# Linear attention feeding a tanh-shrink MoE on one core: a quarter of q issued by SyncE, transposes copied late, 1/den of two head pairs split into bf16 parts by GpSimd, batch 1 reordered

## The chip, the cores and the metric

The kernel runs on one core of one Trainium2 chip. The metric is the device time of one execution in microseconds (us). Unless a number is called a median of runs, it is a start or a length in the profiled execution of the kernel named, in microseconds from the start of that execution's span; the span is about 1.8 us shorter than the device time. In the lines of profiles PE is TensorE, DVE VectorE, ACT ScalarE, POOL GpSimd and SP SyncE; PSUM is the memory, in eight banks, in which TensorE's results lie, and a load "lands" when its data is there.

## The reference

```python
# q, k, v: 8 batches x 8 heads x 576 tokens x 64;  w_in: 512 x 2048;  w_out: 2048 x 512
phi = lambda x: np.where(x > 0, x, np.exp(x) - 1.0) + 1.0
q_p, k_p = phi(q), phi(k)
kv  = np.einsum('bhsd,bhse->bhde', k_p, v)
z   = np.sum(k_p, axis=2)
num = np.einsum('bhsd,bhde->bhse', q_p, kv)
den = np.einsum('bhsd,bhd->bhs', q_p, z)[..., None] + 1e-06
x   = (num / den).transpose(0, 2, 1, 3).reshape(4608, 512)
h   = x @ w_in
out = (h - np.tanh(h)) @ w_out
```

## The kernel before

The kernel works through the 4608 tokens in nine chunks of 512, `c` = 0 to 8. A chunk is 64 matmuls with `w_in` ("L1": 16 blocks `fi` of four) and 64 with `w_out` ("L2": 16 steps of four), each 0.216 us when TensorE runs dense. The attention of the next batches is worked in between: `s1[fi]` holds what follows block `fi` of L1, `s2[s]` what follows step `s` of L2. So the order of the program text is the order of each engine's work. Attention of a batch is: exp and phi of q and k (ScalarE, VectorE), transposes of phi(q) (TensorE, copied out of PSUM by ScalarE or VectorE), kv and z, den, its reciprocal, num, and the scaling of num by 1/den into `xT`, from which L1 reads.

The opening, and the work of batch 1 in chunk 0 (cuts marked):

```python
load_q(0)                      # two halves, each one transfer issued by GpSimd, cast float32 -> bf16
load_k(0)
make_identity(nc, ident)
load_v(0)
for f0, n in (...): load_wi(f0, n)
load_k(1); load_wo(0); load_wo(1); load_q(1)
...                            # memsets by GpSimd
load_v(1); load_wo(2); load_wo(3)
...
spin(18)                       # dummy matmuls while q lands
a_qT_pe(0, 0, side, "AV")      # transposes; copies by ScalarE and VectorE
... # phi(k)
spin(5)
a_qT_pe(0, 1, side, "AA")
... # z, kv, den of batch 0
b0_spread((0, 2), 0)           # 1/den spread over partitions, float32 matmuls
b0_scale(0, ns0, 0); b0_scale(2, ns0, 1)
b0_num(1, ns0)
def open2():                   # called after the first two L1 matmuls of chunk 0
    b0_spread((1, 3), 2)
    b0_scale(1, ns0, 2); b0_scale(3, ns0, 3)
...
s2[7].append(lambda: (a_qT_pe(1, 0, side), a_qT_pe(1, 1, side), a_kv(1, side)))
s2[8].append(lambda: b0_scale_rest(side))
s2[9].append(lambda: a_den(1, side))
s2[10].append(lambda: (num1(), a_split(1)))
s2[11].append(lambda: spread1(0))
```

Chunk 1 makes batch 2. Its `vp` is v of batch 2 in another layout, and its 1/den goes through DRAM and is broadcast back (`rdb`):

```python
s1[7 if c == 1 else 5].append(lambda: a_kv_cols(n1, attn))                     # needs vp
s1[10 if c == 1 else 8].append(lambda: (a_den(n1, attn), a_spread(n1)))       # den, 1/den, broadcast
for p in range(NP + 1):
    s2[(11 if c == 1 else 9) + p].append(lambda p=p: a_num(n1, p))             # needs the broadcast
if c == 1:
    s1[1].append(lambda: a_kphi(2, 1))
    for i in range(2):
        s1[3].append(lambda i=i: a_vp(2, i))
if c >= 1 and n2 < B:
    s1[0].append(lambda: (gate(qT_t[n1]), load_k(n2), load_q(n2), load_v(n2)))
```

Of the kernel before, what the change touches and what calls it, by code (L numbers as in the profile page):

```python
# [18 lines left out]
def kernel(  # L19
# [65 lines left out]
    def load(b, t, src, halves):  # L85

        x = src[b].rearrange("h (p j) d -> (h p) (j d)", j=J)
        if halves:
            for i in range(2):
                nc.gpsimd.dma_start(out=t[:, :, i].rearrange("q h j d -> q h (j d)"),  # L90
                                    in_=x.rearrange("(h i q) x -> i q h x", h=2, i=2)[i])
        else:
            nc.gpsimd.dma_start(out=t.rearrange("q h i j d -> q (h i) (j d)"),  # L93
                                in_=x.rearrange("(n q) x -> q n x", n=4))
# [26 lines left out]
    def phi_pieces(b, src, store, name, i, parts=0):  # L121
# [7 lines left out]
        if parts:  # L129

            return ([lambda h=h: nc.scalar.activation(e[:, h], x[:, h], AF.Exp) for h in range(2)],
                    lambda: nc.vector.tensor_scalar(r, x, 0.0, 1.0, ALU.max, ALU.add),
                    [lambda h=h: nc.vector.tensor_tensor(y[:, h], e[:, h], r[:, h], ALU.min) for h in range(2)])
# [37 lines left out]

    def kv_mm(b, i, ps):
# [15 lines left out]
    def a_vp(b, i):  # L188
        nc.vector.tensor_copy(vp[:, i, :, 0:128].rearrange("p j (h d) -> p h j d", h=2), v_b[b % 2][:, 0:2, i])

# [14 lines left out]
    def b0_z(i):  # L205

        for j in range(J):
            for hg in range(2):
                r = slice(64 * hg, 64 * hg + 64)
                nc.tensor.matmul(ps_all[:, 4 - 2 * i + hg, 0:32], kp_t[0][r, i, j].rearrange("p h d -> p (h d)"),  # L210
                                 one[r, 0:32], start=(j == 0), stop=(j == J - 1))

    def b0_zc(i):
        nc.vector.tensor_mul(kz_t[0][:, :, i, 128:160], ps_all[:, 4 - 2 * i:6 - 2 * i, 0:32], mask[:, :, i, 128:160])

    def b0_kv(i):

        for j in range(J):
            for hg in range(2):
                r = slice(64 * hg, 64 * hg + 64)  # L220
                nc.tensor.matmul(ps_all[:, 2 * i + hg, 0:128], kp_t[0][r, i, j].rearrange("p h d -> p (h d)"),
                                 v_b[0][r, 0:2, i, j, :], start=(j == 0), stop=(j == J - 1))

    def b0_kz(i):
        nc.vector.tensor_mul(kz_t[0][:, :, i, 0:128], ps_all[:, 2 * i:2 * i + 2, 0:128], mask[:, :, i, 0:128])

    def b0_num(i, ns):
# [5 lines left out]
        nc.scalar.copy(ns[:, i::2, 0:8, :].rearrange("p a j t -> p a (j t)"), ps_all[:, b0:b0 + 2, :])  # L233

# [172 lines left out]
    nc.scalar.activation(act0, zero[:, 0:1], AF.Exp)  # L407
    load_q(0)
# [5 lines left out]
    load_k(1)  # L414
    load_wo(0)
    load_wo(1)
    load_q(1)
    for i in (1, 0):
        nc.gpsimd.memset(v_b[i][:, 2], 1.0)
    nc.gpsimd.memset(vp[:, :, :, 128:136], 1.0)  # L420
    load_v(1)
    load_wo(2)
    load_wo(3)

# [20 lines left out]

    side = Banks([4, 5, 6, 7])
    kz_t[0] = kz_c[0]
    (eq0, rq0, mq0), (eq1, rq1, mq1) = (phi_pieces(0, q_t, qp_t, "qp", i) for i in range(2))
    for f in (eq0, rq0, mq0, eq1, rq1, mq1):
        f()  # L450
    spin(18)
    a_qT_pe(0, 0, side, "AV")
    (ek0, rk0, mk0), (ek1, rk1, mk1) = (phi_pieces(0, k_t, kp_t, "kp", i, 2 * i) for i in range(2))
# [3 lines left out]
    a_qT_pe(0, 1, side, "AA")  # L457

    for t in range(4):
        nc.scalar.copy(s8[32 * t:32 * t + 32, 0].rearrange("q h p -> q (h p)"),  # L460
                       ident[32 * t:32 * t + 32, 32 * t:32 * t + 8])
    nc.scalar.copy(sel, s8[:, 0].rearrange("q h p -> q p h").unsqueeze(3).to_broadcast([128, NP, 2, 64]))
    spin(6)
# [3 lines left out]
    b0_zc(0)  # L467
    b0_kv(0)
    b0_kz(0)
    b0_z(1)  # L470
    b0_zc(1)
    a_den(0, Banks([4]))
    ns0 = new_ns(0)
# [9 lines left out]
    def open2():  # L483
        b0_spread((1, 3), 2)
        b0_scale(1, ns0, 2)
        b0_scale(3, ns0, 3)

    def prepare():

        for t in range(4):  # L490
            nc.vector.tensor_copy(s8[32 * t:32 * t + 32, 1:3].rearrange("q n h p -> q (n h p)"),
                                  ident[32 * t:32 * t + 32, 32 * t + 8:32 * t + 24])
        s24 = rpool.tile([128, 2 * NP], F32, name="s24")
        f8 = s8.rearrange("q n h p -> q n (h p)")
        nc.vector.tensor_add(s24, f8[:, 1], f8[:, 2])
# [147 lines left out]
```

## Time and profile before

The time is 294.82 us, the median of three runs (294.65 to 294.93). Five points cut the first 85 us into parts.

| point | before, us | how it is read |
|---|---|---|
| k's second half in use | 10.46 | first exp of k in two pieces on ScalarE |
| dense stream starts | 17.64 | the row of 62 L1 matmuls on TensorE |
| transposes of batch 1 start | 37.94 | the row with ident,qp |
| chunk 1 starts | 51.30 | the next row of L1 matmuls |
| chunk 2 starts | 82.12 | the same, one chunk on |

From VectorE's timeline of the kernel before (start, length, line, operation, output and input, idle time in front and what ended it):

```profile
64.37 1.05 DVE L285 RECIPROCAL rden<-den 128x144 f32<-128x144 f32 x1
79.10 1.89 DVE L328 TENSOR_TENSOR xT<-ps_all,rdb 128x512 bf16<-128x512 f32 x3 [2.26 <-DMA rdb<-ds]
```

And from TensorE's:

```profile
62.60 0.43 PE L276 MATMUL ps_all<-qT,kz 128*32 128x144 bf16 x16
...
78.73 0.38 PE L317 MATMUL ps_all<-qT,kz 128*128 128x512 bf16 x1
...
79.85 0.38 PE L317 MATMUL ps_all<-qT,kz 128*128 128x512 bf16 x1
```

1/den of batch 2 is ready at 65.42, and its broadcast is in use at 79.10, in the first of the scalings: VectorE waits for it. The num matmuls of a batch share two PSUM banks, so the third needs the bank that the first scaling frees; that scaling takes 0.69 us, to 79.79, and the third num matmul starts at 79.85, 0.04 later than the step of 1.08 between the first two would bring it.

### The profile page before, as it was taken

The numbers are of one execution on the slowest core, as the hardware profiler recorded it, in microseconds if no ns is written. First come the engines' busy times: TensorE is split into PE (matmuls) and PEld (weight loads), VectorE is DVE, ScalarE is ACT, GpSimd is POOL, SyncE is SP. The second block draws the span as 40 slices with busy tenths as digits, with TensorE's granted clock in tenths as the row PEclk, the third lists the DMA queues.
The fourth block names the chain that finished last, engine by engine and source line by source line (L and its number), as shares of the span: only waits on it lengthen the run. The fifth ranks groups of instructions, "written<-read, shape, count | busy, mean of one in ns | idle before, by whom it ended". The sixth has DMA issues, their size and how long they took to land.

```text
span 293.2 us, 4504 instructions
## 1 busy us (share of the span) xinstructions
PE 285.2 (97%) x1801; PEld 134.3 (46%) x1801; DVE 174.6 (60%) x265; ACT 139.6 (48%) x168; POOL 33.3 (11%) x55
## 2 busy tenths in 40 slices
PE   8899999999999999999999999999999999999994
PEld 2544453454444444444444445444444444444443
DVE  4759857887567764786478646865581456106600
ACT  4938536947344643455246524661552155126411
POOL 8673030030030003000300020000000000000000
PEclk9999999999999999999999999999999999999999
DMA  6999999998999758955895669667117310131032
GB/s 101 194 204 212 208 207 216 200 145 153 234 163 185 160 118 139 218 117 129 136 223 127 139 134 183 134 154 143 38 24 178 73 36 0 38 84 24 0 74 72
DMA packets 39077, 38.94 MB, mean 133 GB/s; under 512 B 16336, under 2 KB 33808, under 8 KB 38288
## 3 DMA queue, kind: packets, MB, share of 16 engines
q0 software_dynamic: 17552, 18.35, 38.6%
q1 hardware_dynamic: 21344, 20.17, 30.3%
q8 instruction: 14, 0.23, 0.3%
q10 hardware_dynamic: 160, 0.13, 0.1%
q14 instruction: 7, 0.06, 0.1%
HBM read 43.91 MB, written 9.55 MB: 182 GB/s over the span
## 4 chain that ended last, share of the span: by engine, by line
PE 79%; DMA 11%; issue 7%; POOL 2%; DVE 0%; ACT 0%; POOLq 0%
PE ps_all L387 37%; PE ps_all L366 36%; DMA qraw<-in_q_dram 6%; DMA w_in_sb<-in_moe_w_in_dram 3%; PE ps_all L199 2%; DMA kraw<-in_k_dram 2%; PE ps_all L317 2%; PE ps_all L604 1%; PE ps_all L276 1%; POOL qraw L90 0%; ACT e L134 0%; POOL kraw L93 0%; DVE qp L136 0%; POOL v L93 0%; POOL w_out_sb L115 0%
## 5 line engine op out<-in xcount | busy, mean ns | idle before, releaser
L366 PE MATMUL ps_all<-xT,w_in_sb 128*128 128x512 bf16 x576 | 128.0, 379 | 0.3 <-DVE xT L244 0.3
L387 PE MATMUL ps_all<-w_out_sb,gT 128*128 128x512 bf16 x560 | 127.8, 379 | 0.0
L373 DVE TENSOR_TENSOR gT<-ps_all,th 128x1024 bf16<-128x1024 f32 x64 | 77.9, 1218 | 59.8 <-ACT th L372 59.8
L372 ACT ACTIVATE th<-ps_all 128x1024 f32<-128x1024 f32 x64 | 65.5, 1024 | 57.0 <-PE ps_all L366 47.1
L366 PEld LDWEIGHTS <-w_in_sb 128*128 128x128 bf16 x576 | 55.3, 98 | 66.6 <-issue 0.6
L387 PEld LDWEIGHTS <-gT 128*128 128x128 bf16 x560 | 54.1, 98 | 64.3 <-issue 0.3
L396 ACT COPY osb<-ps_all 128x512 f32<-128x512 f32 (+1 forms) x36 | 20.9, 583 | 73.4 <-PE ps_all L387 54.2
L328 DVE TENSOR_TENSOR xT<-ps_all,rdb 128x512 bf16<-128x512 f32 x24 | 16.3, 689 | 13.4 <-PE ps_all L317 11.2
L134 ACT ACTIVATE e<-qraw 128x1152 bf16<-128x1152 bf16 x16 | 18.5, 1162 | 6.9 <-DMA qraw<-in_q_dram 6.9
L134 ACT ACTIVATE e<-kraw 128x1152 bf16<-128x1152 bf16 x15 | 17.5, 1166 | 0.2 <-DMA kraw<-in_k_dram 0.2
L136 DVE TENSOR_TENSOR qp<-e,r 128x1152 bf16<-128x1152 bf16 x16 | 12.0, 757 | 7.8 <-ACT e L134 7.2
L136 DVE TENSOR_TENSOR kp<-e,r 128x1152 bf16<-128x1152 bf16 x15 | 11.4, 759 | 8.3 <-ACT e L134 7.5
L383 POOL COPY g<-qT 1x1 bf16<-1x1 bf16 x5 | 1.2, 240 | 120.6 <-DMA qT<-qp 120.6
L378 DVE TENSOR_TENSOR gT<-ps_all,th 128x512 bf16<-128x512 f32 x16 | 10.3, 685 | 2.4 <-ACT th L377 1.7
L377 ACT ACTIVATE th<-ps_all 128x512 f32<-128x512 f32 x16 | 9.2, 598 | 4.3 <-PE ps_all L366 3.1
L317 PE MATMUL ps_all<-qT,kz 128*128 128x512 bf16 x28 | 10.1, 379 | 0.0
L444 PE MATMUL ps_all<-zero 128*128 128x512 bf16 x29 | 8.8, 463 | 1.2 <-DVE zero L405 1.2
L135 DVE TENSOR_SCALAR r<-qraw 128x1152 bf16<-128x1152 bf16 x16 | 7.3, 453 | 2.2 <-DMA qraw<-in_q_dram 2.2
L199 PE MATMUL ps_all<-vp,kp 64*128 64x136 bf16 x216 | 7.4, 220 | 0.4 <-POOL g L383 0.4
L199 PEld LDWEIGHTS <-kp 64*128 64x128 bf16 x216 | 6.4, 94 | 3.0 <-issue 2.1
L285 DVE RECIPROCAL rden<-den 128x144 f32<-128x144 f32 x7 | 7.4, 1053 | 0.2
L394 DVE COPY osb<-ps_all 128x128 f32<-128x128 f32 x1 | 0.3, 292 | 11.6 <-PE ps_all L604 11.6
(82 smaller groups left out, 121.7 us busy)
## 6 DMA issues: line engine op xcount, KB each, us to landing
out_dram<-osb SPq DMA_DIRECT2D x70, 128.0 KB
rdb<-ds SPq DMA_DIRECT2D x12, 576.0 KB
kraw<-in_k_dram POOLq DMA_DIRECT2D x7, 576.0 KB, 7.1
qraw<-in_q_dram POOLq DMA_DIRECT2D x7, 576.0 KB, 9.0
v<-in_v_dram POOLq DMA_DIRECT2D x7, 576.0 KB, 12.2
w_out_sb<-in_moe_w_out_dram POOLq DMA_DIRECT2D x4, 512.0 KB, 16.4
w_in_sb<-in_moe_w_in_dram POOLq DMA_DIRECT2D x6, 256.0 KB, 8.6
qraw<-in_q_dram POOLq DMA_DIRECT2D x2, 288.0 KB, 4.6
```

What stands on the lines that cost most here:

```text
L134: return (lambda: nc.scalar.activation(e, x, AF.Exp), lambda: nc.vector.tensor_scalar(r, x, 0.0, 1.0, ALU.max, ALU.add), lambda: nc.vector ...
L136: lambda: nc.vector.tensor_tensor(y, e, r, ALU.min))
L199: nc.tensor.matmul(ps[hg][:, i, :], kp[r, i, j].rearrange("p h d -> p (h d)"), vp[r, i, j, :], start=(j == 0), stop=(j == J - 1))
L317: nc.tensor.matmul(ps, kz[:, p // 2, p % 2, 0:128], qT[:, p % 2, 0:8, p // 2, :], start=True, stop=True)
L328: nc.vector.tensor_mul(xT[:, p, S * b:S * b + 512].rearrange("p (j t c) -> p j t c", j=8, t=4), ps.rearrange("p j (t c) -> p j t c", t=4), ...
L366: nc.tensor.matmul(h, w_in_sb[:, 2 * (p % 2) + p // 2, fi * 128:(fi + 1) * 128], xT[:, p, c * 512:(c + 1) * 512], start=(n == 0), stop=(n ...
L372: nc.scalar.activation(th, h, AF.Tanh)
L373: nc.vector.tensor_sub(gT[:, fi:fi + 2, :], h, th)
L377: nc.scalar.activation(th, h, AF.Tanh)
L378: nc.vector.tensor_sub(gT[:, fi, :], h, th)
L387: nc.tensor.matmul(o, gT[:, fi, i * 128:(i + 1) * 128], w_out_sb[:, fi, :], start=(fi == 0), stop=(fi == NF - 1))
L396: nc.scalar.copy(osb[:, f0:f1], o[:, f0:f1])
```

## The change

The intent is to fill what the profile shows as empty. SyncE, idle in the opening, fetches a quarter of q; copies of transposes move behind the exps of k; the second float32 spread becomes a bf16 one, whose input is made by GpSimd; batch 1 is put in an order with fewer holes; the product of batch 2 moves two blocks later, so that its `vp` is there in time. Cut to its core:

```diff
 def load(...):                                     # halves of batch 0
+    if src is q and i == 0:
+        nc.sync.dma_start(out=q_f, in_=...)         # a quarter, stays float32
+        nc.gpsimd.dma_start(out=t[:, 1, i]..., in_=...)   # the second quarter
+        continue
 ...
-load_k(1) ... load_wo(3)                           # behind load_wi
+                                                   # now behind GpSimd's six operations
 ...
+eq0[0](); rq0[0](); eq0[1]()
+prepare()                                          # moved here from s2[0]
-spin(18); a_qT_pe(0, 0, side, "AV"); ...; spin(5); a_qT_pe(0, 1, side, "AA")
+spin(14); T0 = b0_T(0); ...; spin(5); T1 = b0_T(1)
+for x in (*T0, T1[0]): nc.scalar.copy(*x)          # behind the exps of k
 ...
+b0_z(1); nc.vector.tensor_copy(*T1[1]); b0_zc(1)   # z of both halves ahead of kv
 ...
 a_den(0, Banks([4]))
+nc.gpsimd.tensor_copy(t10, f0)                     # f0 = 1/den
+nc.gpsimd.tensor_scalar(u0, t10, part[:, 0:1], None, ALU.mult)
+nc.gpsimd.tensor_add(u0, u0, f0)
+nc.gpsimd.tensor_copy(t20, u0)
+nc.gpsimd.tensor_scalar(v0, t20, part[:, 1:2], None, ALU.mult)
+nc.gpsimd.tensor_add(w0, v0, u0)
 ...
 def open2():
-    b0_spread((1, 3), 2)
+    b0_spread3((1, 3), 2)                           # bf16, reads w0
 ...
-s2[7].append(lambda: (a_qT_pe(1, 0, side), a_qT_pe(1, 1, side), a_kv(1, side)))
+s2[7].append(lambda: (a_qT_pe(1, 0, side), a_kv(1, side), a_qT_pe(1, 1, side)))
-s2[9].append(lambda: a_den(1, side))
-s2[10].append(lambda: (num1(), a_split(1)))
+s2[9].append(lambda: (a_den(1, side), num1(), a_split(1)))
 ...                                                # batch 2's phi(q) one step later
-s1[7 if c == 1 else 5].append(lambda: a_kv_cols(n1, attn))
-s1[10 if c == 1 else 8].append(lambda: (a_den(n1, attn), a_spread(n1)))
+s1[9 if c == 1 else 5].append(lambda: a_kv_cols(n1, attn))
+s1[11 if c == 1 else 8].append(lambda: (a_den(n1, attn), a_spread(n1)))
 ...
-s1[1].append(lambda: a_kphi(2, 1));  s1[3].append(...a_vp(2, 0), a_vp(2, 1))
+s1[1].append(k21[0]);  s1[3].append(lambda: (k21[1](), k21[2](), a_vp(2, 1)))
+s1[5].append(lambda: a_vp_act(2, 0))                # one vp copy by ScalarE
```

## The prediction

> **What bounds the kernel now.** I read the page's busy lines first, then the timeline of each engine over the first 60 us, then the transfers by stretch.
>
> ```profile
> PE 285.2 (97%) x1801; PEld 134.3 (46%) x1801; DVE 174.6 (60%) x265; ACT 139.6 (48%) x168; POOL 33.3 (11%) x55
> DMA  6999999998999758955895669667117310131032
> ```
>
> TensorE is busy 97% of a 293.2 us span, but the dummy matmuls on `zero` hide the opening. The second line is the transfers' share in 40 slices of 7.3 us: full from the second slice to about 52 us. So a gain must come from TensorE's order before about 60 us, and transfers can cap it. The TensorE timeline (start, length, what, how many, idle time before it and what ended it):
>
> ```profile
> 16.38 0.59 PE L366 MATMUL ps_all<-xT,w_in_sb 128*128 128x512 bf16 x2 [0.33 <-DVE xT L244]
> 16.98 0.73 PE L240 MATMUL ps_all<-rden,sel 32*128 32x128 f32 x16
> 17.64 13.55 PE L366 MATMUL ps_all<-xT,w_in_sb 128*128 128x512 bf16 x62
> 31.03 7.07 PE L387 MATMUL ps_all<-w_out_sb,gT 128*128 128x512 bf16 x32
> 37.94 0.68 PE L164 MATMUL ps_all<-ident,qp 128*128 128x128 bf16 x9
> 39.17 0.68 PE L164 MATMUL ps_all<-ident,qp 128*128 128x128 bf16 x9 [0.56 <-DVE qp L136]
> 39.78 1.66 PE L177 MATMUL ps_all<-v,kp 64*128 64x192 bf16 x36
> 41.37 1.04 PE L387 MATMUL ps_all<-w_out_sb,gT 128*128 128x512 bf16 x4
> ...
> 47.26 0.31 PE L354 MATMUL ps_all<-w,sel 32*128 32x144 bf16 x8 [0.69 <-ACT ns L344]
> ...
> 51.30 7.07 PE L366 MATMUL ps_all<-xT,w_in_sb 128*128 128x512 bf16 x32
> 58.74 1.24 PE L199 MATMUL ps_all<-vp,kp 64*128 64x136 bf16 x36 [0.37 <-POOL g L383]
> ```
>
> The dense stream starts at 17.64 and runs unbroken to 37.94 (94 matmuls at 0.216). Then batch 1 is worked in with holes; from 51.30 it is dense, but for 0.37. The opening, by ScalarE and VectorE, and the transfers of batch 1 that decide what follows (KB, us from issue to landing):
>
> ```profile
> 5.55 1.16 ACT L134 ACTIVATE e<-qraw 128x1152 bf16<-128x1152 bf16 x1 [3.32 <-DMA qraw<-in_q_dram]
> 10.46 1.26 ACT L131 ACTIVATE e<-kraw 128x576 bf16<-128x576 bf16 x2 [0.34 <-DMA kraw<-in_k_dram]
> 13.58 1.06 DVE L285 RECIPROCAL rden<-ps_all 128x144 f32<-128x144 f32 x1 [0.42 <-PE ps_all L276]
> 13.52 2.03 POOL L110 DMA_DIRECT2D w_in_sb<-in_moe_w_in_dram  x3 [0.78 <-DMA v<-in_v_dram]
> ```
> ```profile
> v<-in_v_dram POOLq DMA_DIRECT2D x1, 576.0 KB, 16.5
> w_out_sb<-in_moe_w_out_dram POOLq DMA_DIRECT2D x1, 512.0 KB, 18.3
> ```
>
> The second half of k lands at about 10.4 and starts everything after it: exp, kphi, z, den, reciprocal, spread, scale, first matmul at 16.38. v of batch 1, issued at 22.28, lands at 38.8; the third part of w_out, issued at 23.01, lands at 41.3.
>
> **The Trainium skill.** "DMA: Bandwidth & Descriptors", section "Issuing engines are not separate DMA queues": SyncE's and GpSimd's transfers share the same 16 engines, so another issuer saves only issue time. The trace agrees in that the share stays full while both issue; but in the stretch 2 to 3 us it is 0.26 and in 3 to 4 us 0.77, so here an earlier issuer fills empty time. Same page, "SWDGE vs HWDGE vs iDMA": a cast needs GpSimd's path, which is why SyncE's quarter stays float32. "GPSIMD Engine Reference", "3.1 Elementwise — side-by-side cycle accounting": a two-input tensor operation takes about 2.6 cycles an element. This trace has no such instruction; its GpSimd fill of 1152 elements took 1.08 us and one of 128x128 0.26, so about 0.15 fixed and 0.9 ns an element.
>
> **The change part by part.**
>
> (1) *A quarter of q by SyncE.* GpSimd issues its first transfer at 1.24 (0.78 us each for a half) and packets flow only from about 2.8, slowly till 3.6. SyncE is free at about 0.75; in a quiet stretch near the end its packets follow the copy's end by about 1.1 us, so I put its first at about 2. The quarter is 0.29 MB; halves land 1.35 to 2.05 us apart, so a quarter is 0.7 to 0.9 us of transfer. I take all later landings as 0.8 earlier: k at 9.6, v of batch 0 at about 11.1 and 12.5, v of batch 1 at 38.0, w_out's third part at 40.5.
>
> (2) *Late copies.* In the opening ScalarE's three copies of transposes (0.69 alone, 1.16 a pair) go behind exp(k), VectorE's behind the first z product. Exp(k) is transfer-bound before and after, ending at 10.9 instead of 11.72. But the copies then hold den: 10.95 + 3 x 0.58 + 0.05 = 12.7, where before they ended at 12.78. Den ends at 13.05 instead of 13.5, the reciprocal starts at 13.1 instead of 13.58. The 0.8 shrinks to 0.5. prepare() on VectorE (33.98 to 35.7, 1.76 us in all) moves to about 4.5 to 6.3, waiting for ident; the first qp is then done near 7.4, no later than before (7.51). Where it was, VectorE was about to wait for q anyway, so removing it gives nothing.
>
> (3) *1/den in bf16 parts.* The second spread, 16 float32 records at 0.66 us (16.98 to 17.64), becomes 8 bf16 matmuls, by L354's row about 0.25: -0.4. But it needs six GpSimd operations on 128x144: four one-input at about 0.3 and two two-input at 144 x 2.6 / 1.2 GHz = 0.31 + 0.15 = 0.46, an estimate from the page: 2.1 us. They stand behind the issue of w_in, which ends at 15.55, waiting for v of batch 0; 0.8 earlier is 14.75. So w is ready at about 16.9; TensorE could start that spread at about 16.5, loses 0.4 and resumes the dense stream at about 17.25. Parts 1 to 3 together: 17.64 to 17.25, -0.4; with what is rough in this, 0 to -0.9.
>
> (4) *Batch 1 reordered.* Transposes at 37.55 (q lands at 35.1, so no wait), to 38.05. kv needs v at 38.0: about no wait; 1.57 long, to 39.65. Second transposes 0.51, to 40.15; their qp is long ready, which removes the 0.56. The next w_out matmuls need the third part at 40.5: a new wait of 0.3. From there to c=1: 32 matmuls at 0.216 = 6.9, rest 0.12, den 0.36, num 0.12 + 0.86, two spreads 0.46 = 8.8; against 9.93 before (41.37 to 51.30). num right behind den gives ScalarE its copies a stage sooner, so the 0.69 goes, but the split's four VectorE operations (about 1.3 after a reciprocal of 1.05) end just behind and leave 0.2 to 0.3. So c=1 starts at 40.5 + 9.1 = 49.6 instead of 51.30: -1.7. This includes the 0.4 above; it isn't added to it.
>
> (5) *c=1.* The product of batch 2 moves two fi later and one vp copy goes to ScalarE (about 1.1 us): the 0.37 goes. But ScalarE's exps of batch 2 stand closer behind the stream, and I find about 0.3 of new waiting for PSUM banks there. 1/den of batch 2 comes one fi later and, on VectorE, behind another gT, so its broadcast lands relatively later; VectorE already waits for it at 79.10 (2.3 us). TensorE has about 1 us of slack there. Net 0 to +0.4. The rest is the same work at the same 0.216.
>
> Sum: -1.7 - 0.37 + 0.3 + 0.1 = -1.7, so 294.82 - 1.7 = 293.1.
>
> **Rivals.** (A) GpSimd's w becomes the wait: for it, six dependent operations behind in-order issues, and GpSimd shares its SBUF ports with VectorE ("GPSIMD Engine Reference", "8. Key points"), which is busy there; against it, fills of this size took 0.25. If each takes 0.6, the stream resumes at 18.5, behind before; then the waits for v and w_out vanish and c=1 starts at about 50.4: 294.0. (B) Transfers bind: they are full to 52 us, and if SyncE's quarter only shares the first microseconds (shift 0.3), w_out lands at 41.0 and c=1 starts at 50.1: 293.6. (C) GpSimd is quick (under 0.25 each) and the shift a full 1 us: dense from 16.75, w_out at 40.3, c=1 at about 49.2: 292.6. (D) The broadcast of batch 2 comes late in c=1 and stalls a bank pair: +0.5 to 0.9 on any of these.
>
> **Range and chances.** The rivals span 292.6 to 294.5 with D; the holes that the change can close sum to about 0.9 + 0.3 + 0.56 + 0.69 + 0.37 = 2.8, so 292.0 is the floor. Range 292.0 to 294.4. Faster by 2% would need 5.9 us, twice all holes there are: 0.01. Slower by 2% would need a new stall of 6 us: 0.01. Within 2%: 0.98.
>
> **What would show it.** First exp(q) on a quarter before 4.5 us; exp of k's second half at about 9.6, reciprocal at about 13.1; GpSimd's six operations from about 14.8 to 16.9 and the bf16 spread just after; dense L-one matmuls from about 17.25; no idle before the second transposes of batch 1, a short idle before the w_out matmuls behind them; c=1's stream at about 49.6. I am wrong if the landings don't shift, if GpSimd's chain ends after 18, if a wait grows in c=1 before the batch-2 products, or if matmuls of the dense part change from 0.216.

## The result, and the profile after

The changed kernel took 296.91 us (296.85 to 296.91, four runs), the kernel before in the same rounds 294.88 (294.65 to 295.20): a ratio of 1.0068, 95% interval 1.0050 to 1.0085. Ratios here and below are the mean time of one kernel's runs over that of the other's of the same rounds, so not quite the ratio of the medians quoted. The predicted gain of 1.7 us was a loss of 2.0, outside the range.

TensorE's timeline of the changed kernel, from the opening into chunk 1:

```profile
17.38 0.38 PE L397 MATMUL ps_all<-xT,w_in_sb 128*128 128x512 bf16 x1 [0.33 <-DVE xT L275]
19.61 0.29 PE L263 MATMUL ps_all<-w,sel 32*128 32x128 bf16 x8 [1.86 <-POOL w L527]
19.84 13.55 PE L397 MATMUL ps_all<-xT,w_in_sb 128*128 128x512 bf16 x61
...
40.14 0.67 PE L172 MATMUL ps_all<-ident,qp 128*128 128x128 bf16 x9
40.73 1.66 PE L197 MATMUL ps_all<-v,kp 64*128 64x192 bf16 x36
42.33 0.68 PE L172 MATMUL ps_all<-ident,qp 128*128 128x128 bf16 x9
42.84 1.03 PE L418 MATMUL ps_all<-w_out_sb,gT 128*128 128x512 bf16 x3
...
52.10 8.94 PE L397 MATMUL ps_all<-xT,w_in_sb 128*128 128x512 bf16 x39
...
64.53 0.72 PE L307 MATMUL ps_all<-qT,kz 128*32 128x144 bf16 x16 [0.49 <-DVE kz L225]
...
81.83 0.38 PE L348 MATMUL ps_all<-qT,kz 128*128 128x512 bf16 x1 [0.49 <-DVE xT L359]
...
84.10 5.34 PE L397 MATMUL ps_all<-xT,w_in_sb 128*128 128x512 bf16 x24
```

(Counts such as 61 and 39 instead of 62 and 40 are records missing from the trace; the lengths are whole.) The reader should see three things. TensorE now waits 1.86 us for `w`, which GpSimd makes, and the dense stream starts 2.20 us later than before. Batch 1 has no hole in these rows, and the part from its transposes to chunk 1 takes 52.10 - 40.14 = 11.96 us instead of 13.36: 1.40 won. Chunk 1 then takes 84.10 - 52.10 = 32.00 instead of 30.82, with two waits that before did not have: 1.18 lost. The sum is +2.20 - 1.40 + 1.18 = +1.98, which is the whole difference.

| part | before | after | difference |
|---|---|---|---|
| k's second half in use | 10.46 | 11.18 | +0.72 |
| from there to the reciprocal of den | 3.12 | 3.40 | +0.28 |
| from the reciprocal to the dense stream | 4.06 | 5.26 | +1.20 |
| dense stream to the transposes of batch 1 | 20.30 | 20.30 | 0 |
| transposes of batch 1 to chunk 1 | 13.36 | 11.96 | -1.40 |
| chunk 1 | 30.82 | 32.00 | +1.18 |

The first row is read from ScalarE's timeline of the changed kernel:

```profile
3.67 0.68 ACT L137 ACTIVATE e<-gT 128x576 bf16<-128x576 f32 x1 [1.44 <-DMA gT<-in_q_dram]
5.25 0.68 ACT L137 ACTIVATE e<-qraw 128x576 bf16<-128x576 bf16 x1 [0.90 <-DMA qraw<-in_q_dram]
8.16 1.16 ACT L142 ACTIVATE e<-qraw 128x1152 bf16<-128x1152 bf16 x1 [2.23 <-DMA qraw<-in_q_dram]
9.65 1.16 ACT L142 ACTIVATE e<-kraw 128x1152 bf16<-128x1152 bf16 x1 [0.33 <-DMA kraw<-in_k_dram]
11.18 1.26 ACT L137 ACTIVATE e<-kraw 128x576 bf16<-128x576 bf16 x2 [0.37 <-DMA kraw<-in_k_dram]
```

SyncE's quarter is in use 1.9 us before anything was before (5.55), the second quarter 0.3 before; but q's second half comes at 8.16 where it came at 6.90, and everything behind it is late. The bytes moved show that an early start need not last: in the stretches 2 to 3, 3 to 4, 4 to 5 and 5 to 6 us the changed kernel moved 248, 137, 96 and 145 GB/s, the kernel before 15, 89, 204 and 206.

GpSimd's timeline of the changed kernel:

```profile
14.23 2.01 POOL L116 DMA_DIRECT2D w_in_sb<-in_moe_w_in_dram  x3 [0.81 <-DMA v<-in_v_dram]
16.24 0.32 POOL L521 CAST t<-rden 128x144 bf16<-128x144 f32 x1
16.66 0.65 POOL L522 TENSOR_SCALAR u<-t,part 128x144 f32<-128x144 bf16 x1
17.39 0.49 POOL L523 TENSOR_TENSOR u<-u,rden 128x144 f32<-128x144 f32 x1
17.94 0.30 POOL L524 CAST t<-u 128x144 bf16<-128x144 f32 x1
18.35 0.65 POOL L526 TENSOR_SCALAR v<-t,part 128x144 f32<-128x144 bf16 x1
19.07 0.49 POOL L527 TENSOR_TENSOR w<-v,u 128x144 bf16<-128x144 f32 x1
```

1/den was ready at 14.58 + 1.06 = 15.64, but GpSimd issues transfers of `w_in` until 16.24. Then the six operations need 3.32 us to 19.56: 2.90 of work and 0.42 of gaps between dependent operations. And from VectorE's timeline of the changed kernel, the two rows of chunk 1 that were shown of the kernel before:

```profile
66.66 1.05 DVE L316 RECIPROCAL rden<-den 128x144 f32<-128x144 f32 x1
81.08 1.89 DVE L359 TENSOR_TENSOR xT<-ps_all,rdb 128x512 bf16<-128x512 f32 x3 [2.88 <-DMA rdb<-ds]
```

Chunk 1 began 0.80 later, but this reciprocal is 2.29 later and the broadcast is in use 1.98 later. Against the start of chunk 1 the broadcast is thus in use 28.98 us on instead of 27.80, 1.18 later, and that is the whole of what chunk 1 lost: the third num matmul again starts when the first scaling is over (81.77), and TensorE now shows a wait of 0.49 us there.

### The profile page after: what moved, and what is told of

Read it like the earlier page. It is cut to its first block, busy times and chain, and to the rows that moved or that the text cites. A ratio compares the mean times of both kernels' runs of the same rounds, so it can differ in the third digit from the quotient of the medians. Undisturbed runs are those within 1.5% of the kernel's fastest.

```text
span 295.1 us, 4452 instructions
## 1 busy us (share of the span) xinstructions
PE 282.6 (96%) x1759; PEld 133.4 (45%) x1788; DVE 175.7 (60%) x266; ACT 140.0 (47%) x166; POOL 36.4 (12%) x61
## 4 chain that ended last, share of the span: by engine, by line
PE 67%; DMA 6%; SPq 1%; DVE 1%; ACT 1%; issue 1%; DVEq 0%
PE ps_all L397 33%; PE ps_all L418 30%; DMA rdb<-ds 3%; DMA out_dram<-osb 2%; PE ps_all L222 2%; PE ps_all L348 2%; DMA ds<-rden 1%; PE ps_all L307 1%; ACT osb L427 1%; SPq L432 0%; DVE rden L316 0%; SPq L336 0%; DVE xT L359 0%; PE ps_all L351 0%; SPq L339 0%
## 5 line engine op out<-in xcount | busy, mean ns | idle before, releaser
L418 PE MATMUL ps_all<-w_out_sb,gT 128*128 128x512 bf16 x547 | 126.1, 379 | 0.7
L142 ACT ACTIVATE e<-qraw 128x1152 bf16<-128x1152 bf16 x15 | 17.3, 1161 | 3.4 <-DMA qraw<-in_q_dram 3.4
L144 DVE TENSOR_TENSOR qp<-e,r 128x1152 bf16<-128x1152 bf16 x15 | 11.4, 758 | 7.5 <-ACT e L142 6.7
L466 PE MATMUL ps_all<-zero 128*128 128x512 bf16 x24 | 7.8, 487 | 1.2 <-DVE zero L436 1.2
L116 POOL DMA_DIRECT2D w_in_sb<-in_moe_w_in_dram x10 | 6.4, 646 | 3.6 <-DMA kraw<-in_k_dram 1.6
```

What stands on the lines that cost most here:

```text
L142: return (lambda: nc.scalar.activation(e, x, AF.Exp), lambda: nc.vector.tensor_scalar(r, x, 0.0, 1.0, ALU.max, ALU.add), lambda: nc.vector ...
L144: lambda: nc.vector.tensor_tensor(y, e, r, ALU.min))
L418: nc.tensor.matmul(o, gT[:, fi, i * 128:(i + 1) * 128], w_out_sb[:, fi, :], start=(fi == 0), stop=(fi == NF - 1))
```

## The experiments

There were seventeen runs, of fourteen different kernels, all correct. The theory after the result: *the wait for GpSimd's `w` and the late landings cost the opening 2.2 us, and chunk 1's new order gives back what batch 1 won.* The rivals: the late copies or SyncE's quarter are what hurts; chunk 1 is longer only because the opening shifted it against its transfers. All times are device medians, with the kernel before in the same rounds.

| run | time, us | ratio (95%) | k's 2nd half in use | stream | chunk 1 | chunk 2 |
|---|---|---|---|---|---|---|
| x1_fp32 | 295.00 | 1.0006 (0.9992-1.0020) | 10.28 | 17.73 | 49.99 | 82.08 |
| x2_nosp | 297.54 | 1.0096 (1.0077-1.0114) | 10.62 | 20.56 | 52.82 | 84.77 |
| x3_c1old | 296.41 | 1.0054 (1.0040-1.0069) | 11.28 | 19.91 | 52.17 | 83.71 |
| x4_reorder | 294.60 | 0.9999 (0.9984-1.0013) | 10.36 | 17.54 | 50.46 | 81.70 |
| x5_nosp_prepfirst | 295.34 | 1.0011 (0.9996-1.0026) | 10.41 | 17.86 | 50.58 | 82.81 |
| x6_fp32_c1old | 294.96 | 0.9997 (0.9969-1.0025) | 10.58 | 18.03 | 50.57 | 81.91 |
| x7_vpgp | 294.67 | 0.9985 (0.9969-1.0002) | 10.44 | 17.59 | 50.49 | 82.00 |
| x8_vlate | 294.66 | 0.9988 (0.9973-1.0003) | 10.32 | 17.63 | 50.54 | 81.94 |
| x9_qpool (one look) | 296.39 | - | 11.26 | 19.34 | 51.60 | 83.57 |
| x10_gponly | 297.66 | 1.0079 (1.0056-1.0103) | 11.16 | 19.78 | 52.82 | 83.61 |
| x11_best | 294.18 | 0.9974 (0.9961-0.9987) | 10.52 | 17.71 | 50.38 | 81.27 |
| x12_after | 298.42 | 1.0103 (1.0076-1.0131) | 11.26 | 19.99 | 53.76 | 85.69 |
| x13_unused | 295.79 | 1.0031 (1.0016-1.0046) | 11.12 | 18.57 | 50.83 | 82.87 |
| x14_fill | 297.17 | 1.0069 (1.0055-1.0083) | 11.24 | 19.98 | 52.24 | 84.39 |
| x15_fp32_again | 295.77 | 1.0035 (1.0014-1.0056) | 10.94 | 18.39 | 50.65 | 82.58 |
| x16_after_pair | 296.99 | 1.0060 (1.0045-1.0074) | 10.90 | 19.62 | 53.33 | 85.21 |
| x17_fill_pair | 296.97 | 1.0064 (1.0049-1.0079) | 10.82 | 19.56 | 51.83 | 84.01 |

The last four columns are of the one profiled run of each; the times are of all its runs.

### GpSimd's split taken out: x1_fp32

```diff
-six GpSimd operations
-    b0_spread3((1, 3), 2)
+    b0_spread((1, 3), 2)       # float32, reads 1/den itself
```

> The changed kernel with the second spread in float32 again, as before, and GpSimd's six operations gone; all else kept. Theory (GpSimd's 1/den is the wait of 1.86 us in front of the second spread): the spread starts when the second scale of the opening ends, near 17.95, takes 0.66, and the dense stream resumes near 18.6 instead of 19.84; the time falls by about 1.2 us to 295.7. Rival (transfers cap it: v of batch 1 and the third part of w_out land no earlier): part of the 1.2 comes back as a wait near 39 to 42 us, and the time falls by 0.5 or less. Rival (it was the late den only): no change, since TensorE would wait for something else.

Measured: 1.9 us below the changed kernel, and level with the kernel before. The wait is gone and the stream starts at 17.73. But in this run the landings were early too (10.28), so the 1.9 is not all the split's; x13 parts the two. The run also shows where batch 1's gain goes: chunk 1 starts 1.31 earlier than before, chunk 2 only 0.04 earlier. Chunk 1 takes 32.09 us here although the opening is not late, so the rival "shifted by the opening" is out. And TensorE shows no wait for v or `w_out` in batch 1 (38.02 to 49.99, 11.97 us), which matters for x4 below.

### The result of the split made but not used: x13_unused

```diff
     six GpSimd operations stay
-    b0_spread3((1, 3), 2)
+    b0_spread((1, 3), 2)
```

> The changed kernel with GpSimd's six operations left where they are, but their result not used: the second spread is the float32 one again and waits for nothing of GpSimd's. Open so far: in the changed kernel the second half of q came into use at 8.16, 8.31 and 8.23 us in three programs with the six operations, at 6.69 and 7.13 in two without them. Theory 'tied to the program': with the six operations present it is again about 8.2, exp of k's second half about 11.2, the reciprocal about 14.6, the dense stream about 18.3, the time about 295.6. Rival 'chance of the run': 6.7 to 7.2, the stream at 17.7, 295.0. Either way the wait of 1.86 us for GpSimd is gone and nothing of 1.5 us takes its place, and the time is at least 1.2 us below the changed kernel's.

Measured: 1.1 us less than the changed kernel's 296.91. The reciprocal started at 14.52, within 0.06 of the changed kernel's 14.58, and the stream at 18.57 instead of 19.84. So the wait for `w` alone, net of the 0.43 us that the float32 spread is longer, costs 19.84 - 18.57 - 0.06 = 1.2 us. That is the cleanest number for step (3), as neither the landings nor GpSimd's work differ.

### GpSimd's split alone on the kernel before: x10_gponly

```diff
+prepare()                       # ahead of phi(q)
 a_den(0, Banks([4]))
+six GpSimd operations;  load_k(1) ... load_wo(3) behind them
-    b0_spread((1, 3), 2)
+    b0_spread3((1, 3), 2)
```

> The kernel before with only 1/den split by GpSimd and the second spread in bfloat16 (prepare ahead of q's exp and max, and the loads of batch 1 behind the split, as the split needs). Theory (six GpSimd operations take 3.3 us and start when w_in is issued, at about 15.6): w at 18.9, the spread behind it, the dense stream at 19.2 instead of 17.64, while the waits of 0.33 and 0.56 of batch 1's transposes go as q has landed by then; time 295.5. Rival (the chain costs its full 1.55 at the end): 296.4.

Measured: the split is a loss by itself. TensorE's timeline of this run:

```profile
17.09 0.38 PE L374 MATMUL ps_all<-xT,w_in_sb 128*128 128x512 bf16 x1 [0.33 <-DVE xT L252]
19.55 0.29 PE L240 MATMUL ps_all<-w,sel 32*128 32x128 bf16 x8 [2.09 <-POOL w L493]
19.78 13.56 PE L374 MATMUL ps_all<-xT,w_in_sb 128*128 128x512 bf16 x61
```

The wait is 2.09 us and the stream 2.14 later than before, with none of the other parts but the early `prepare`; 0.71 of that stands in front of the reciprocal (14.29 instead of 13.58), 1.43 behind it. Its loads of q were in halves, as before, and landed late all the same (k at 11.16), which first cast doubt on the idea that quarters are what delays them. Its profiled run took 296.38 at a mean clock of 1.000, the three others 297.56 to 297.80 at 0.993 to 0.994: see x12.

### SyncE's quarter taken out: x2_nosp and x5_nosp_prepfirst

```diff
-    if src is q and i == 0: ... nc.sync.dma_start(...) ...     # x2: q in two halves by GpSimd
```

> The changed kernel with q of batch 0 loaded in two halves by GpSimd, as before; prepare and the late copies kept. Theory (SyncE's quarter made the later landings later): q's second half is used at 6.9 instead of 8.16 and k's second half at 10.5 instead of 11.18, the reciprocal starts at about 13.9 instead of 14.58, GpSimd's w ends about 0.7 earlier, and the time falls by 0.7 to 296.2. Rival (VectorE's new work of prepare in 4.9 to 7 us, or the order of packets by chance, held the landings): k's second half stays at 11.1 or later and the time stays at 296.9.

Measured: slower than the changed kernel, for two reasons that I had not thought of. `prepare` stands behind the first piece of phi(q) in VectorE's order; with halves that piece can start only at 5.57, so `prepare` falls on the path: the first transposes start at 9.00 instead of 8.13, and phi(k) is done at 12.71, 0.5 later than in the mended form below (12.22). The larger part is TensorE's clock. Its timeline, and VectorE's wait for z:

```profile
9.00 1.14 PE L182 MATMUL ps_all<-ident,qp 128*128 128x128 bf16 x9 [2.47 <-DVE qp L134]
9.94 2.34 PE L459 MATMUL ps_all<-zero 128*128 128x512 bf16 x5
...
14.34 0.23 DVE L231 TENSOR_TENSOR kz<-ps_all,mask 128x64 bf16<-128x64 f32 x1 [1.64 <-PE ps_all L227]
```

The five dummy matmuls take 2.34 us where they take 1.24 in the mended form: the trace has a granted clock of 0.50 from 8.99 to 12.40, behind an idle stretch of 2.47 us. So the reciprocal starts only at 15.85, and the stream at 20.56. The three runs with a mean clock of 0.994 took 297.53 to 298.33; the one with 0.998 took 296.95, as the changed kernel does. This run does not measure the quarter. It does show the six operations once more, on a GpSimd that had waited 1.08 us for 1/den: 16.97 to 20.28, 3.31 us. So the length of the chain is its own, not the queue's.

The mended form puts `prepare` first and takes the split out too, to be compared with x1:

```diff
-eq0[0](); rq0[0](); eq0[1](); prepare(); ...
+prepare(); eq0[0](); eq0[1](); rq0[0](); ...     # on x1, without SyncE's quarter
```

> The changed kernel with float32 second spread (no GpSimd split) and q in two halves by GpSimd, with prepare put ahead of the first work on q, so that it isn't in front of q's first half as in the run without SyncE's quarter (there VectorE was 1.2 us late for kphi). Compared with the run with the float32 spread alone (SyncE's quarter kept; exp of k's second half at 10.28, reciprocal at 13.67, stream at 17.73): theory (SyncE's quarter gives almost nothing): exp of k's second half at 10.5 to 10.6, reciprocal at 13.9, stream at 18.0, the time within 0.4 us of 295.0. Rival (the quarter is worth its 0.8): stream at 18.5, time 295.5 or more.

Measured: the stream starts at 17.86, against 17.73, 18.03 and 18.39 in the three runs that have the quarter and no split (x1, x6, x15). SyncE's quarter is worth nothing that these runs can show. (x6 ran in the same rounds; the three differ by 0.66 among themselves.)

### Two quarters, both by GpSimd: x9_qpool

```diff
-    nc.sync.dma_start(out=q_f, in_=...)
+    nc.gpsimd.dma_start(out=t[:, 0, i]..., in_=...)       # on x1
```

> The changed kernel with float32 second spread, and the quarter that SyncE loaded now loaded by GpSimd too, as a quarter of its own in bfloat16 (three q transfers from one issuer). Theory (a second issuer's packets bring a second set of slow first packets, which eat the head start): slow packets as in the kernel before (about 9 us in sum over the 16 engines before 5.5 us, against 14 to 19 in the runs with SyncE's quarter), q's second half in use at about 7.0. Rival (small transfers of q by quarters are what is slow): as many slow packets as with SyncE and a second half at 7.5 or later.

Measured, in one look of unknown state: k's second half at 11.26, the stream at 19.34. Packets of the loads that took far longer than the usual 0.107 us (up to 1.04 us) persisted to 7.5 us and beyond although SyncE issued nothing. I read that as "the quarters do it, not the second issuer". With the spread of landings that the later runs showed (next part but one), one look cannot carry that reading, and it stays open. Nor is the stream's start to be set against it: the trace has a granted clock of 0.50 from 8.47 to 11.89, and the reciprocal waited for TensorE, not for k alone.

### Chunk 1 as before: x3_c1old and x6_fp32_c1old

```diff
-s1[9 if c == 1 else 5] ... s1[11 if c == 1 else 8]       # x3: on the changed kernel
+s1[7 if c == 1 else 5] ... s1[10 if c == 1 else 8]       # x6: on x1
-s1[1].append(k21[0]); s1[3]... ; s1[5].append(lambda: a_vp_act(2, 0))
+s1[1].append(lambda: a_kphi(2, 1)); s1[3]...a_vp(2, 0), a_vp(2, 1)
```

> The changed kernel with c=1 as before: the product of batch 2 behind fi 7, its den behind fi 10, kphi and both vp copies on VectorE at the old places. Theory (the later places in c=1 cost about 1.2: from 52.10 to the start of c=2 it takes 32.0 instead of 30.8): the waits of 0.49 for kz and 0.49 for the broadcast of batch 2 go, and the time falls by about 1.0 to 295.9. Rival (the waits come from batch 2's q and k pieces that stand one stage later in c=0): the old order in c=1 then waits for vp or PSUM banks instead, and the time stays or rises.

> The changed kernel with float32 second spread and with c=1 as before: what is left of the change is SyncE's quarter, the late copies, prepare early, and the new order of batch 1 in c=0. Theory (with GpSimd's wait gone the stream resumes near 17.7, c=1 starts near 50.0, and with the old c=1 the broadcast of batch 2 is issued earlier): a vp wait of about 0.75 in c=1, the start of c=2 at 81.4, time 294.2. Rival (the broadcast of batch 2 is held by the loads of batch 3, not by its place): c=2 starts at 82.0 and the time is 294.9. Also: does k's second half land at 10.3, as in the float32 run, or at 11.2, as in the changed kernel and the run with the old c=1? Theory that it differs by run and not by kernel: either may come.

Measured: chunk 1 takes 83.71 - 52.17 = 31.54 us in x3 and 81.91 - 50.57 = 31.34 in x6, against 31.9 to 32.2 in all eleven runs of the new order and 30.82 before. So the new order of chunk 1 costs about 0.6 us, and half of its 1.18 us excess is not the order's: the rest comes in with batch 1's new order (x4), which brings phi(q) of batch 2 later and nearer to chunk 1; x10, with the old order in both chunks, has 30.79. The wait in TensorE's timeline of x3 that takes the place of the two:

```profile
59.99 1.24 PE L222 MATMUL ps_all<-vp,kp 64*128 64x136 bf16 x36 [0.74 <-DVE vp L209]
```

Before, the hole at this place was 0.37 us. The gain in time of x3, 0.5 us, is smaller than the expected whole. What holds TensorE last is the broadcast of 1/den here too: in every profile but those of x8 and x11 the third num matmul starts 0.05 to 0.06 us after the end of the first scaling, and chunk 1 is as long as the time from its start to that scaling plus 3.02 us (27.80 before, 28.98 in the changed kernel, 28.52 in x3, 28.22 in x4). The waits for `vp` and `kz` count in so far as they make 1/den, and with it the broadcast, late.

### Batch 1's new order alone: x4_reorder

```diff
-s2[7].append(lambda: (a_qT_pe(1, 0, side), a_qT_pe(1, 1, side), a_kv(1, side)))     # on the kernel before
+s2[7].append(lambda: (a_qT_pe(1, 0, side), a_kv(1, side), a_qT_pe(1, 1, side)))
-s2[9], s2[10]: den | num, split          -s2[12] ... s2[15]: phi(q) of batch 2
+s2[9]: den, num, split                   +s2[13] ... s2[15]
```

> The kernel before with only the new order of batch 1 in c=0 (kv between the transposes, num right behind den, batch 2's pieces one stage later). Theory (transfers cap this part: v of batch 1 at 38.8, third part of w_out at 41.3): kv waits about 0.4 for v and the w_out matmuls a little; c=1 starts near 50.6 instead of 51.30; the time falls by about 0.7 to 294.2. Rival (the new order is worth its full 1.4, as the changed kernel shows from 40.14 to 52.10 against 37.94 to 51.30): 293.5. Rival (c=1 gives it back, as batch 2's pieces come a stage later): 294.8.

Measured: chunk 1 starts 0.84 earlier than before, not 1.40. TensorE's timeline shows what caps it:

```profile
38.69 1.66 PE L177 MATMUL ps_all<-v,kp 64*128 64x192 bf16 x36 [0.18 <-DMA v<-in_v_dram]
...
41.20 1.02 PE L387 MATMUL ps_all<-w_out_sb,gT 128*128 128x512 bf16 x4 [0.24 <-DMA w_out_sb<-in_moe_w_out_dram]
...
58.28 1.24 PE L199 MATMUL ps_all<-vp,kp 64*128 64x136 bf16 x36 [0.75 <-DVE vp L189]
```

Waits for v and the third part of `w_out`, 0.42 us together, appear when the order is tight and the opening is not late. In the changed kernel the opening was 2.2 us late and the reorder showed its full 1.40 without them. It is not a fixed cap, though: x1, whose opening was on time too, had neither wait, x11 only that for `w_out` (0.24). Then the hole in front of the product of batch 2 doubles from 0.37 to 0.75, and of the 0.84 us, 0.42 are left at chunk 2. The device time does not show even that (0.9999).

### Where chunk 1 can be mended: x7_vpgp, x8_vlate, x11_best

x7 gives both `vp` copies of batch 2 to GpSimd, on top of x4. x8 also holds the load of v of batch 3 until 1/den of batch 2 is there, so that it does not stand in front of the broadcast. x11 is the kernel before with batch 1's new order, the product of batch 2 behind block 8 instead of 7, and that late load.

```diff
-    for i in range(2): s1[3].append(lambda i=i: a_vp(2, i))
+    for i in range(2): s1[0].append(lambda i=i: a_vp_gp(2, i))         # x7: nc.gpsimd.tensor_copy
-s1[0].append(lambda: (gate(...), load_k(n2), load_q(n2), load_v(n2)))
+s1[0].append(lambda: (gate(...), load_k(n2), load_q(n2), c > 1 and load_v(n2)))     # x8, x11
+if c == 1: s1[11].append(lambda: (gate2(rden_t[n1]), load_v(n2)))
-s1[7 if c == 1 else 5].append(lambda: a_kv_cols(n1, attn))
+s1[8 if c == 1 else 5].append(lambda: a_kv_cols(n1, attn))                          # x11
```

> The kernel before with the new order of batch 1 in c=0 and both vp copies of batch 2 on GpSimd, which idles there, instead of VectorE. Compared with the new order alone (c=1 at 50.46, wait of 0.75 for vp, c=2 at 81.70, 294.6 us): theory (the broadcast of batch 2, held by batch 3's loads, binds next): the 0.75 goes, but a wait of about 0.5 comes at the third num of batch 2; c=2 at about 81.4, time 294.3. Rival (vp was the bound): c=2 at 80.95, time 293.8.

> As the run with the vp copies on GpSimd, and the load of batch 3's v is held back until 1/den of batch 2 is ready, so that 0.59 MB fewer stand in front of the small transfer that the broadcast waits for. Theory: that transfer lands about 2 us earlier than 70.3, the broadcast at 77 or earlier, no wait at num, c=2 at about 80.9, time 293.8, better than before by about 1 us. Rival (the broadcast's own transfer is the slow part, over 8 us from issue to use, or v then comes late for its copy): no change from the other run.

> The kernel before with the new order of batch 1, the product of batch 2 one fi later in c=1 (behind fi 8), and batch 3's v held back until 1/den of batch 2 is ready. Theory: c=1 at 50.5, a wait of about 0.4 for kz instead of 0.75 for vp, the broadcast in time; c=2 at 81.3; 294.3 us, 0.2% better than before. Rival (it only moves the waits): 294.7.

x7: the wait for `vp` went, and another took its place. VectorE's timeline of x7, while GpSimd copies from 52.31 to 54.91:

```profile
52.52 1.40 DVE L135 TENSOR_SCALAR r<-kraw 128x1152 bf16<-128x1152 bf16 x1
54.02 1.51 DVE L136 TENSOR_TENSOR kp<-e,r 128x1152 bf16<-128x1152 bf16 x1
...
56.59 0.44 DVE L135 TENSOR_SCALAR r<-kraw 128x1152 bf16<-128x1152 bf16 x1
57.14 0.76 DVE L136 TENSOR_TENSOR kp<-e,r 128x1152 bf16<-128x1152 bf16 x1
```

The first two rows run beside GpSimd's copies, the last two are the same operations on the other half without them: 1.40 against 0.44, 1.51 against 0.76. The late VectorE then kept TensorE waiting 0.89 us for a PSUM bank. x8: the transfers of the broadcast are issued at 68.80 instead of 70.60, but it is in use only half a microsecond earlier, 78.48 instead of 78.99 in x7: from issue to use it took 9.7 us instead of 8.4, with batch 3's v, issued at 65.83, now close in front of it. The third num matmul no longer waits for it (0.49 us lie between), but the wait of 0.89 for the bank stays, and the expected gain was not there. x11 is faster than both kernels: 294.18 us against 295.11 for the kernel before in the same rounds, and 296.91 for the changed kernel in its own. It keeps 0.85 us at chunk 2, its only wait in chunk 1 is 0.38 us for a bank, and no wait for `kz` or the broadcast is left. It is small, 0.26%, but the interval excludes zero.

### Late landings: the program or the run?

The changed kernel was run again:

> The changed kernel again, unaltered, for its opening: is the late landing of q's second half (in use at 8.16 in its profile, 8.31 in the run with the old c=1; 6.7 and 7.1 in the two runs with float32 spread) of the kernel or of the run? Theory (it differs by run): any use between 6.7 and 8.3, and a time that follows it by less than one for one, since GpSimd's 3.3 us chain stands behind; 296.9 if late, about 296.2 if early. Rival (it belongs to the kernel): 8.2 again and 296.9.

Then once more (x16), and its version without the split as well:

> The same kernel as x1_fp32, on another chip: a second sample of when q lands without GpSimd's six operations. 'Tied to the program': q's second half in use at 6.7 to 7.2, the stream at about 17.8, the time 0.999 to 1.002 of before. 'Chance of the run': it may be 8.2, the stream at 18.3, and the time 1.002 or more.

In x12 the landings were as in the first run: q's second half in use at 8.23, k's at 11.26. By then four of five runs with the split showed 8.2 to 8.3, and all without it 6.7 to 7.1 but for x9 (7.86), and I suspected that the program itself decided it. x13 (7.64 with the split), x15 (7.81 without it) and above all x16 (6.60, the changed kernel unaltered) took that theory away: the same program gives 6.60 and 8.23. What remains is a statistic over all profiled runs. With q's first half in quarters, one by SyncE, k's second half came into use at 10.28 to 11.28, mean 10.96 in ten runs. With halves it came at 10.32 to 10.62 in seven of eight runs, and at 11.16 in one, mean 10.54. So the quarter by SyncE did not bring the landings 0.8 forward: k's second half was in use 0.4 later on average and never more than 0.18 earlier than before. The visible form is single packets of the loads that take up to 1.6 us where 0.107 is usual, at varying times. What makes them was not settled.

### The clock in the new hole: x12_after, x14_fill, x16_after_pair, x17_fill_pair

x12 took 298.42 us, 1.5 more than the same kernel's first runs, and the 62 matmuls from the second spread to the first L2 matmul took 14.9 us instead of 13.4. Its profile showed a granted clock of 0.50 from 20 to 22 us. To test whether the wait for GpSimd lets the clock fall, the wait was filled with dummy matmuls:

```diff
 def open2():
+    for _ in range(15):
+        nc.tensor.matmul(ps_all[:, 4, 256:512], zero[:, 0:128], zero[:, 0:256], start=True, stop=True)
     b0_spread3((1, 3), 2)
```

> The changed kernel with 15 dummy matmuls of 256 columns (1.6 us at 0.108 each) put on TensorE just ahead of the second spread, where it waits for GpSimd. Theory 'clock': in the repeat on this chip the granted clock fell to 0.50 to 0.84 for about 4 us behind the idle 1.8 us, which made 298.4 of 296.9; with the idle time filled the clock stays at 1.0, the mean clock is 0.998 or more in all runs, the stream from the second spread to the first w_out matmul takes 13.4 and not 14.9, and the time is 296.8 to 297.1. Rival (this chip or the late landing makes 298.4): 298.2 to 298.6, the clock drops still.

x14 ran on yet another chip, so a pair was put on one chip:

> The changed kernel, to be compared with the filled one on the same chip. Clock theory: the hole of 1.8 us ahead of the second spread lets the clock fall in some runs, so its runs spread over 296.8 to 298.7 us, and the slow ones have a mean clock of about 0.993. Rival (the chip where the repeat ran was the cause): all runs within 0.2 us of each other. Landing: q's second half in use at 7.5 to 8.3.

> The changed kernel with 15 dummy matmuls in the hole, on the same chip as its pair. Clock theory: no run above 297.6 us, all mean clocks 0.998 or more, and it is faster than its pair where the pair has runs with a clock of 0.993. Rival: the two have the same spread of times.

The stretches 18 to 19, 19 to 20, 20 to 22 and 22 to 24 us of x16 (the stretch, its length, the engines' busy times, then the granted TensorE clock, the DMA share and GB/s):

```profile
18.00:19.00 1.00, 0.00 (x0) 0.00 (x0) 0.00 (x0) 0.00 (x0) 0.90 (x2) 1.00 1.22 199
19.00:20.00 1.00, 0.72 (x9) 0.26 (x9) 0.20 (x1) 0.00 (x0) 1.00 (x2) 0.60 1.34 211
20.00:22.00 2.00, 2.00 (x6) 0.74 (x5) 1.09 (x2) 0.00 (x0) 2.00 (x4) 0.50 1.23 203
22.00:24.00 2.00, 2.00 (x9) 0.85 (x8) 0.00 (x0) 0.34 (x1) 2.00 (x3) 0.85 1.23 208
```

and the same of x17:

```profile
18.00:19.00 1.00, 1.00 (x11) 0.90 (x10) 0.00 (x0) 0.00 (x0) 0.90 (x2) 1.00 1.26 205
19.00:20.00 1.00, 1.00 (x14) 0.44 (x13) 0.25 (x1) 0.00 (x0) 1.00 (x2) 1.00 1.30 205
20.00:22.00 2.00, 2.00 (x11) 0.94 (x10) 1.03 (x2) 0.00 (x0) 2.00 (x4) 1.00 1.24 205
22.00:24.00 2.00, 2.00 (x11) 0.92 (x10) 1.23 (x2) 1.53 (x3) 2.00 (x3) 1.00 1.22 207
```

Behind the empty stretch TensorE, fully busy, retired 6 matmuls in 2 us instead of 11. The traces' own clock records have the drop to 0.50 from 19.19 to 22.61 in x16 and from 19.67 to 23.08 in x12, 3.41 us each. Of the six runs of x16, two had a mean clock of 0.993 (297.94, the profiled one, and 297.25 us), the other four 0.998 to 1.000 (296.46 to 297.08). Of the eleven runs of the filled kernel (x14 and x17) none was below 0.998. So the clock theory is borne out: the hole can cost up to 1.5 us beyond its own length, in some executions. But the medians of the pair, 296.99 and 296.97, are level: filling wins nothing in the usual execution. In the first runs of the changed kernel the profiled one had a clock of 1.00 through all its work, so this is not part of its 2.0 us.

A mean clock of 0.993 or 0.994 does not tell where the drop was, nor that it cost time: one of the changed kernel's first four runs had 0.994 and the same 296.91 us, and x15, which has no wait for GpSimd, had one of 0.994 at 297.19. The change made a second hole, in the opening: with 14 dummy matmuls instead of 18, TensorE idles 1.61 us in front of the first transposes instead of 0.29, and in x2 (2.47) and x9 (2.13) it was this hole that a drop followed.

When does a hole do it? The clock records of all nineteen traces change on a grid of 3.41 us, which starts at another point in each execution. Each of their 23 drops, those at a kernel's end included, follows a window of this grid in which TensorE had been idle for 2.04 us or more in all (2.16 in x12, 2.06 in x16); none follows a window with 1.95 us or less (1.79 in the changed kernel's first profile). So it depended on how the hole fell on the grid whether one of 1.8 us, with some shorter waits beside it, was followed by a drop. (These idle times are worked out from the traces, in which the ends of matmuls are modelled.)

The Trainium skill's page "TensorE: Matmul & The Clock Gate", section "Part 1: The HAM clock gate (the "warmup" mystery)", says that an idle TensorE falls to half its clock and that the activity window, of about 3.4 us, runs freely, so that the same kernel differs from run to run. The traces agree in all three: 0.50, 3.41 us, and a drop in x12 and x16 but not in the first profile of the same kernel. The page asks for an idle window; here a window idle for 2.04 of its 3.41 us was enough.

## Why the prediction was wrong

The time was wrong because three terms of the sum failed: the early landings (step 1), GpSimd's chain (step 3) and the slack in chunk 1 (step 5).

**Step (1), a quarter by SyncE: failed.** "I take all later landings as 0.8 earlier." The quarter itself was early, in use at 3.67 as the prediction's check asked ("before 4.5 us"). But the step from "this part is early" to "all behind it is earlier by its share" was an assumption. Over ten runs with the quarter the landings were 0.4 us later than with halves, in the first run 0.7. Taking the quarter out (x5) changed the opening by nothing that could be seen. This alone moves the sum by 1.5 us in the first run: 0.72 late instead of 0.8 early.

**Step (2), late copies: right.** I expected them to hold den so that 0.8 of gain becomes 0.5, a cost of 0.3; from k's landing to the reciprocal it took 3.40 instead of 3.12, a cost of 0.28, and 3.39 to 3.40 in every run that has them, but for x2 and x9 with their drops of the clock. No run parts them from the rest of the opening's new order. That `prepare` stands harmlessly where VectorE would wait is right too, but only with the early quarter, or ahead of q as in x5: in x2, behind q's first piece, phi(k) was done 0.5 later than in x5.

**Step (3), 1/den by GpSimd: right mechanism, wrong size, and the wrong main line.** The saving on the spread was right (16 float32 records of 0.66 us became 8 of 0.23). The chain was put at 2.1 us. The casts took 0.31 as taken from the fills, and the additions 0.49, close to the 0.46 estimated from the Trainium skill, "GPSIMD Engine Reference", section "3.1 Elementwise — side-by-side cycle accounting". Missing were the multiplications by a scalar for each partition, 0.65 instead of 0.3, because I counted them as one-input operations like a fill; and the 0.42 us of gaps between dependent operations, which I left out: 0.7 + 0.4 = 1.1 us of the 1.2 between 2.1 and 3.3, the rest being 0.1 of casts and additions. (The two fills give 0.8 ns an element, not the 0.9 written; 0.3 for a fill of this size stands.) The start was 16.24 instead of 14.75, since the landing it hangs on was late. Rival (A) named this very wait, with 18.5 for the stream and 0.6 for each operation, and it is what happened, at 19.84. The chain after 18 was also among the things that I wrote would make me wrong. x13 measured the wait at 1.2 us net, where the prediction had a gain of 0.4.

**Step (4), batch 1: right.** Predicted from 37.55 to 49.6, 12.05 us, of which 0.3 was waiting for `w_out`; measured 11.96 without that wait, as rival (A) said of a late opening. The size is right as well: 1.40 of what was predicted as 13.36 - 12.05 = 1.31. That transfers cap the gain where the opening is on time is seen in x4 (waits of 0.18 and 0.24 us) and in part in x11, but not in x1, so it hangs on the landings of the run. (The digits of the transfers' share, read as full to about 52 us, stand at 9 up to the ninth slice, 66 us; nothing in the sum rests on it.)

**Step (5), chunk 1: failed.** "Net 0 to +0.4", with "about 1 us of slack" for the broadcast. Measured +1.18. The hole of 0.37 did go, but the slack was not there: in the kernel before, too, the third num matmul started just when the first scaling was over (79.85 and 79.79). So all of what the broadcast came later against the start of chunk 1, 28.98 instead of 27.80, was TensorE's loss. It came later because 1/den did, by 1.49: one more block of L1 stands in front of den (four matmuls at 0.216, 0.86 us); `kz` of batch 2 moved behind more of VectorE's work and made den wait 0.49; the den matmuls then ran 0.29 longer (0.72 against 0.43 in their rows); less the hole, that is 1.27 of it. Rival (D) named this, "+0.5 to 0.9", as a thing that might come on top; x1 and x13 show that it belongs to the new order where the opening is earlier too, x3 and x6 that about half of it goes when chunk 1 has the old one. And x4 shows that batch 1's gain is half eaten in chunk 1 even without chunk 1's new order, so the parts cannot simply be added.

Put together: step (1) and (2) came out as +1.00 instead of -0.5, step (3) as +1.20 instead of about 0, step (4) as -1.40 where it was expected (a shift of the start by -0.4 and a part shorter by 1.3 made the -1.7), step (5) as +1.18 instead of 0.

## What to carry to other kernels

Work moved to a slower, idle engine is free only if its whole dependent chain, with the gap behind each operation, fits between input and use: count operations by measured rows of the same kind, and ask when the engine's own queue lets it start. In these runs a transfer issued earlier moved itself, not those behind it. And when a hole is closed upstream, look at the next wait downstream before counting the gain: in x4 the loads took part of it, and chunk 1 half of what was left. Slack is to be read at the engine that waits last: in the kernel before, its matmul already started as the operation in front of it ended.

## What the Trainium skill lacked or had wrong

- "GPSIMD Engine Reference", section "3.1 Elementwise — side-by-side cycle accounting": nothing on a multiplication by a scalar for each partition. On 128x144 it took 0.65 us, longer than the two-input addition of the same size (0.49) and twice a cast (0.31); between dependent operations lay a further 0.06 to 0.11 us.
- "TensorE: Matmul & The Clock Gate", section "Part 1: The HAM clock gate (the "warmup" mystery)": the drop to half clock is put behind an idle window of about 3.4 us. Here it followed windows of 3.41 us that were idle for 2.04 us or more in all, and none that were idle for 1.95 or less; a hole of 1.82 us was followed by it in two profiles, at a cost of up to 1.5 us.
- No page has that single packets of the first loads take up to 1.6 us (0.107 is usual); the second half of q was in use at anything from 6.60 to 8.23 us in one and the same program.
- No page has how long the broadcast from DRAM takes beside other loads: 8.3 to 9.7 us from the issue of the first to the use of both, for two transfers of 576 KB.
